# Moving the loads of three head pairs ahead of operand stores, and scaling keys last, in a fused retention and SwiGLU kernel

## The chip, the cores and the metric

The kernel runs on one core of one Trainium2 chip. The metric is the time of one execution on the device, in microseconds (us); lower is better. A core has a matrix engine (TensorE, PE in the profile, with its weight loads as PEld), VectorE (DVE), ScalarE (ACT), GpSimd (POOL) and SyncE (SP), each with its own queue of instructions that is worked off in order. In this kernel DMA transfers of the stage in question are issued from the queues of SP and of ACT.

## The reference

Two blocks, one after the other, all in float32. The first is retention: causal attention without softmax, with a decay per head.

```python
batch, n_heads, seq, head_dim = (8, 8, 576, 64)
scores = (1 / sqrt(64)) * q @ k.T                     # per batch and head
gamma = 1.0 - 2.0 ** (-5.0 - arange(8))               # one decay per head
D[i, j] = gamma ** (i - j) if i >= j else 0
attn = (scores * D) @ v
x = attn.transpose(0, 2, 1, 3).reshape(4608, 512)     # tokens x (heads, dims)
# SwiGLU feed-forward, d_model 512, d_ff 1536
g = x @ w_gate
out = (g * sigmoid(g) * (x @ w_val)) @ w_out          # 4608 x 512
```

## The kernel before

**Retention by pairs.** Two heads of one batch entry make a pair; there are 32 pairs, numbered `i`, four to a batch entry. A pair's sequence is handled in chunks of 64 positions. The work of a pair is spread over three calls of `tick(t)` (L595): at tick t, pair t is transposed and its keys are scaled (`transposes`, L428), pair t-1 gets its scores and states (`scores`, `new_states`, `masked`), and pair t-2 gets its outputs (`own_values`, `earlier_values`, `to_x`). The order of a tick's TensorE work is: `own_values(t-2)`, `new_states(t-1)`, `earlier_values(t-2)`, `scores(t-1)`. `new_states` needs the scaled keys `kn` of its pair, `scores` needs its `qT` and `kT`.

The vector work of a tick is put on a list, `pieces`, and taken off it a few at a time by `go_on(n)`, in this order: copies of the even states together with `keys` (the scaling of the pair's keys), then the outputs, then the mask of the scores, then the states, then the two transposes of `qT` and `kT`. `vector(i)` (L424) is true for pairs 0 and 10 to 12: their keys are scaled on VectorE. For pairs 4 to 9 ScalarE does it.

**Loads.** `load(i)` (L258) issues 13 transfers for a pair from 4 on: four for q and four for k in the layout that the transposes want (`qk`), two for k (`kn`), two for v, one for the last piece of v. They go out on SP's queue, except those of pair 11, which go out on ACT's queue (L267). The buffers rotate: `qk` has two places (`ld`, bufs=2), `kn` three, `v` four, so a load that is emitted waits until an earlier pair has left its place.

**The feed-forward.** Tokens 0 to 511 are computed in the plain way (`up0`, `down0`, `out0`). The other 4096 tokens are four tiles of 1024, and each of their products is done by a fast-matrix-multiplication scheme: three tables (UP, DOWN, OUT_SUMS) list sums and differences of blocks of the operands, 26 block products each, and how the products are added up. The 26 combinations of the weights `w_out` are the same for all tiles, so they are made once and written to DRAM (`dn_ops`, three column groups `qd` 0 to 2 of 26 blocks), and later fetched. This is `out_sums(qd)` (L707): for qd 0 and 1 the sums run on GpSimd and their stores go out on SP's queue; for qd 2 the sums run on VectorE and the stores go out on ACT's queue. A sum is kept in a place out of a short list (six places for GpSimd, six more from f=11 on), and a place is free again when the store of it has landed. `out_sums` returns nine groups of about three stores each.

**The order around the change.** It is written out by hand. A plan runs `up0(f)` for f = 2 to 11, with ticks 4 to 9 after f = 2, 3, 5, 7, 10, 11 (`tick_at`, L978). `next_load(t)` emits `load(t + 2)`. Of the groups of sums for qd 0 and 1, three each follow f = 7, 8, 10 and 11 (L989). Then a loop over twelve `down0` steps, numbered m (L999), runs ticks 10 to 13 after m = 1, 3, 6 and 8, `go_on(4)` in each step, the six groups that are left for qd 1, and the nine groups of qd 2, one for each m from 0 to 8. After m = 8 the sums of the x operands for the first tile of 1024 tokens begin on VectorE (`x_sums`); they need the outputs of pair 11, which come out of tick 13. The tile itself starts with `up_step` (L866) after `out0`.

On SP's queue the order around the change is therefore: load of pair 8, nine stores, load of pair 9, nine stores, load of pair 10, 34 stores. On ACT's queue: the last rounding of weights, the SiLU of `up0(11)`, the copies and keys of tick 9, the load of pair 11, 26 stores for qd 2.

A transfer also waits on one of eight completion counters that the transfers share in the order in which the program was laid out, so that a transfer is issued only when the one eight before it has landed, whichever queue that was on. In the profile such a wait is seen as a store that waits for the landing of a transfer to which it has no other relation.

Of the kernel before, what the change touches and what calls it, by code (L numbers as in the profile page):

```python
# [12 lines left out]
F32 = mybir.dt.float32  # L13
# [3 lines left out]
AF = mybir.ActivationFunctionType  # L17
ALU = mybir.AluOpType
# [136 lines left out]
def kernel(  # L155
# [32 lines left out]
    nc = tc.nc  # L188

    B, H, S, D = q.shape  # L190
    NT, DM = out.shape
    DF = moe_w_gate.shape[1]
    P = 128
    HP = H // 2
# [4 lines left out]
    SQ = 32  # L199
# [3 lines left out]
    NF = DF // P  # L203
# [6 lines left out]
    scale = 1.0 / math.sqrt(D)  # L210
# [4 lines left out]
    ld = ctx.enter_context(tc.tile_pool(name="ld", bufs=2))  # L215
# [26 lines left out]
    rest = const.tile([P, 17920], F32, name="rest")  # L242
# [15 lines left out]
    def load(i):  # L258

        b, p = divmod(i, HP)
        t = kp.tile([P, NFULL, 2, D], F32, tag="v", name="v", bufs=4)
        last = kp.tile([P, D], F32, tag="vl", name="vl", bufs=4)

        queues = (nc.sync, nc.scalar if i < 2 else nc.gpsimd if i < HP else nc.sync)
        if i >= HP and i == needed(1) - 3:  # L267

            queues = (nc.scalar, nc.scalar)

        def chunks(dst, src, hl):
            queues[hl].dma_start(out=dst[:, :, hl, :], in_=src[b, 2 * p + hl, 0:CW, :].rearrange("(c p) d -> p c d", p=P))

        if i < HP:

            late = [rest[:, dn_at + 1280 * (i - 2) + 640 * n :][:, 0:640] for n in range(2)] if i > 1 else None
            flat = late[0] if late else ld.tile([P, 2, S // SQ, SQ], F32, tag="qk", name="qk").rearrange("p n j d -> p (n j d)")
            qk = (flat[:, 0:CW].rearrange("p (c h d) -> p c h d", h=2, d=D),
                  flat[:, CW : CW + P].rearrange("p (h d) -> p h d", h=2))
            kn = (late[1][:, 0:CW].rearrange("p (c h d) -> p c h d", h=2, d=D) if late  # L280
                  else kp.tile([P, NFULL, 2, D], F32, tag="kn", name="kn"))
            for hl in range(2):
                chunks(qk[0], q, hl)
            for n, src in enumerate((q, k)):
                queues[n].dma_start(out=qk[1][half[n]], in_=src[b, 2 * p : 2 * p + 2, CW:S, :].rearrange("h p d -> p h d"))
        else:
            qk = ld.tile([P, 2, S // SQ, SQ], F32, tag="qk", name="qk")
            kn = kp.tile([P, NFULL, 2, D], F32, tag="kn", name="kn")
            for n, src in enumerate((q, k)):
                for a in range(P // SQ):  # L290
                    queues[0].dma_start(
                        out=qk[a * SQ : (a + 1) * SQ, n],
                        in_=src[b, 2 * p + a // 2, :, (a % 2) * SQ : (a % 2 + 1) * SQ].rearrange("(j t) d -> t j d", t=SQ))
        for dst, src in ((kn, k), (t, v)):
            for hl in range(2):
                chunks(dst, src, hl)
        if i < HP:
            for hl in range(2):
                queues[hl].dma_start(out=last[half[hl]], in_=v[b, 2 * p + hl, CW:S, :])
        else:  # L300
            queues[0].dma_start(out=last, in_=v[b, 2 * p : 2 * p + 2, CW:S, :])
        loaded[i] = (qk, kn, t, last)
# [13 lines left out]
    inv, key = tab[:, 0:H], tab[:, H : 2 * H]  # L316
# [103 lines left out]
    def light(i):  # L420

        return needed(1) - 2 <= i < needed(2) - 2

    def vector(i):  # L424

        return i == 0 or 10 <= i <= needed(1) - 2

    def transposes(i):  # L428
        p = i % HP
        qk, kn, vt, last = loaded.pop(i)  # L430
        qT = qp.tile([P, S], F32, tag="qT", name="qT")
        st[i] = dict(qT=qT, kn=kn, v=vt, last=last)
        pieces = []

        copy = nc.scalar.copy if i else nc.vector.tensor_copy
        if i < HP:

            for t, src, bank in ((qT, qk[0], bankA), (kT, kn, bankB)):
                for c in range(NFULL):
                    nc.tensor.transpose(bank[:, ts(c, P)], src[:, c].rearrange("p h d -> p (h d)"), ident)  # L440
                copy(t[:, 0:CW], bank)
            nc.tensor.transpose(bankC[:, 0:P], qk[1].rearrange("p h d -> p (h d)"), ident)
            for n, t in enumerate((qT, kT)):
                copy(t[:, CW:S], bankC[:, n * L : (n + 1) * L])
        else:
            if light(i):
                def scale_q():

                    src = qk[:, 0].rearrange("p (j r) d -> p r j d", r=2)
                    for r in range(2):  # L450
                        nc.scalar.activation(out=src[:, r], in_=src[:, r], func=AF.Copy, scale=piece[:, 2 * p + r : 2 * p + r + 1])
                pieces.append(scale_q)
            for n, t in enumerate((qT, kT)):
                pieces.append(lambda n=n, t=t: nc.vector.transpose(out=t, in_=qk[:, n].rearrange("p j d -> p (j d)")))

        def keys():
            for hl in range(2):
                if vector(i) or 1 < i < HP:
                    (nc.vector if vector(i) else nc.gpsimd).tensor_scalar(out=kn[:, :, hl, :], in0=kn[:, :, hl, :],
                                            scalar1=key[:, 2 * p + hl : 2 * p + hl + 1], scalar2=None, op0=ALU.mult)  # L460
                else:
                    nc.scalar.activation(out=kn[:, :, hl, :], in_=kn[:, :, hl, :], func=AF.Copy,
                                         scale=key[:, 2 * p + hl : 2 * p + hl + 1])

        if light(i):
            return [lambda: (keys(), pieces[0]())] + pieces[1:]
        return [keys] + pieces
# [125 lines left out]
    pieces = []  # L593
# [42 lines left out]
    def go_on(n):  # L636
        for _ in range(min(n, len(pieces))):
            pieces.pop(0)()

    def needed(n):  # L640

        last = (min(starts[n] + TW, NT) - 1) // S
        return last * HP + HP - 1 + 3
# [4 lines left out]
    def up0(f, chunks):  # L648

        pair = banks[2 * (f % 2) : 2 * (f % 2) + 2]  # L650
        for gv, bank in enumerate(pair):
            for c in chunks:
                nc.tensor.matmul(bank, w_up[:, f // 4, gv, f % 4, c // 2, (c % 2) * P : (c % 2 + 1) * P], xs[0][:, c, :],  # L653
                                 start=(c == 0), stop=(c == HP - 1))
        if HP - 1 in chunks:
            s = io[:, (f % 2) * T0 : (f % 2 + 1) * T0]
            nc.scalar.activation(out=s, in_=pair[0], func=AF.Silu)
            nc.vector.tensor_tensor(out=hid0[f], in0=pair[1], in1=s, op=ALU.mult)
# [43 lines left out]
    for line in OUT_SUMS:  # L702
        i, s = line.split("|")
# [259 lines left out]
    def next_load(t):  # L963
        if t + AHEAD < NP:
            load(t + AHEAD)
# [4 lines left out]
    plan = []  # L970

    def round_until(i):
        while todo and order.index(i) >= todo[0]:
            m = todo.pop(0)
            plan.extend(lambda j=j: rounding(j) for j in (2 * m, 2 * m + 1))

    round_until(3)
    tick_at = {2: 4, 3: 5, 5: 6, 7: 7, 10: 8, 11: 9}  # L978
    for f in range(2, NF):
        round_until({4: 12, 6: 13, 8: 14, 9: 15, 10: 16, 11: 17}.get(f, f + 2))  # L980
        plan.append(lambda f=f: up0(f, range(HP)))
        if f - 1 in tick_at and f < NF - 1:
            plan.append(lambda t=tick_at[f - 1]: next_load(t))
        if f in tick_at:
            plan.append(lambda t=tick_at[f]: tick(t, HP, FIRST))
        if f >= NF - 2:

            plan.append(lambda t=tick_at[f]: next_load(t))
        for _ in range(0 if f == 9 else 3):  # L989
            if f >= (7, 10, NF)[groups[0][0]]:  # L990
                if f + 1 == NF and more_places:
                    plan.append(lambda places=more_places[:6]: pool_places.extend(places))
                    more_places.clear()
                plan.append(lambda group=groups.pop(0)[1]: group())
# [3 lines left out]
    tick_at = {1: 10, 3: 11, 6: 12, 8: 13}  # L998
    for m, f in enumerate(down_order):  # L999
        down0(f)  # L1000
        go_on(4)
        if m in tick_at:
            tick(tick_at[m], HP, FIRST, tick_at[m] + 1 < needed(1))
            go_on(1)
        if m == 8:
            first_sums(0, 0, 4)
        if m > 8:
            x_sums(1, 3 * (m - 9), min(3 * (m - 8), X_FIRST), True)
        if groups:
            groups.pop(0)[1]()  # L1010
        if last_groups:
            last_groups.pop(0)()
# [58 lines left out]
```

## Time and profile before

| | |
|---|---|
| time, median of 3 runs | 1072.69 us (1072.22 to 1075.32) |
| span of the profiled execution | 1071.5 us |
| PE busy | 1040.9 us, 97% |
| DVE busy | 662.0 us, 62% |
| POOL busy | 394.4 us, 37% |
| ACT busy | 272.1 us, 25% |
| DMA packets under 512 B | 215352 of 300700 |

A share of busy time is over the whole span. PE is busy almost always, so the few places where it is not are what can be gained. The profile gives for each engine a timeline in which equal instructions are merged (start, duration, engine, line, what it writes and reads, count, and in brackets the idle time before it with what ended it), and the chain of work that ended last. A name such as `SPq L740` is a DMA issue from SP's queue; `DMA dn<-rest` is the transfer itself, here a store of a sum. `L689` is the line of the adds in the helper `add`, and is shared by all sums; what it writes tells which they are: `rest<-rest 128x256` are sums for w_out.

### The profile page before, as it was taken

What the parts mean: (1) busy time and instruction counts of PE and PEld (TensorE: products, weight loads), DVE (VectorE), ACT (ScalarE), POOL (GpSimd) and SP (SyncE); (2) the same over time, 40 slices, a digit from 0 to 9 for tenths busy, and PEclk for the clock granted to TensorE, in tenths of its full rate; (3) what the DMA queues carried; (4) which work ended last, traced back from release to release, by engine and by line L of the source; (5) the groups of instructions that cost most, each with busy time, mean ns of one, the idle gap of its engine ahead of it and who ended that gap; (6) DMA issues with size and microseconds to landing.
All of it is one profiled execution on the core that took longest, in us unless ns stands there. A gap on an engine that the chain in (4) does not pass through costs nothing.

```text
span 1071.5 us, 21458 instructions
## 1 busy us (share of the span) xinstructions
PE 1040.9 (97%) x8420; PEld 853.9 (80%) x8420; DVE 662.0 (62%) x1093; ACT 272.1 (25%) x578; POOL 394.4 (37%) x345
## 2 busy tenths in 40 slices
PE   6999989999999999999999999999999999999998
PEld 5454544788788788888888888888888888888887
DVE  4568777876968757562657868526276555244644
ACT  3555400224343220223222112132221022221110
POOL 5002454466464304731225026513150384123505
PEclk9999988999999999999999999999999999999999
DMA  9899797546676968756757777554564555555653
GB/s 255 235 264 247 199 234 201 171 148 200 162 205 179 255 173 223 213 180 182 192 133 225 186 223 206 154 153 134 155 176 150 158 180 154 150 155 155 189 157 99
DMA packets 300700, 198.58 MB, mean 185 GB/s; under 512 B 215352, under 2 KB 244056, under 8 KB 300600
## 3 DMA queue, kind: packets, MB, share of 16 engines
q1 hardware_dynamic: 264486, 155.75, 54.2%
q10 hardware_dynamic: 35698, 40.58, 11.4%
q8 instruction: 67, 1.10, 0.5%
q0 software_dynamic: 416, 0.89, 0.3%
q14 instruction: 33, 0.27, 0.1%
HBM read 157.04 MB, written 40.11 MB: 184 GB/s over the span
## 4 chain that ended last, share of the span: by engine, by line
PE 83%; DVE 5%; DMA 4%; POOL 3%; issue 1%; SPq 1%; ACT 0%; DVEq 0%; ACTq 0%; POOLq 0%
PE bankC L882 11%; PE bankE L882 11%; PE bankB L882 11%; PE bankA L882 11%; PE bankA L921 6%; PE bankE L921 6%; PE bankB L921 6%; PE bankC L921 6%; DVE rest L822 2%; PE bankA L653 2%; PE bankC L653 2%; PE bankB L653 2%; PE outer L504 2%; PE bankE L653 2%; POOL rest L689 1%; DMA dn<-rest 1%
## 5 line engine op out<-in xcount | busy, mean ns | idle before, releaser
L822 POOL TENSOR_TENSOR rest<-rest 128x512 f32<-128x512 f32 x56 | 79.1, 1419 | 299.5 <-DVE rest L822 278.4
L897 ACT ACTIVATE io<-rest 128x256 f32<-128x256 f32 x180 | 74.9, 416 | 340.9 <-DVE rest L822 294.8
L689 POOL TENSOR_TENSOR arena<-arena 128x512 f32<-128x512 f32 (+1 forms) x72 | 115.2, 1613 | 45.2 <-DMA up<-arena 24.4
L882 PE MATMUL bankC<-rest,arena 128*128 128x256 f32 x544 | 129.2, 381 | 0.5 <-DVE rest L822 0.5
L882 PE MATMUL bankA<-rest,arena 128*128 128x256 f32 x544 | 128.9, 380 | 0.4 <-DVE rest L822 0.4
L882 PE MATMUL bankE<-rest,arena 128*128 128x256 f32 x512 | 121.5, 380 | 0.6 <-DVE rest L822 0.6
L882 PE MATMUL bankB<-rest,arena 128*128 128x256 f32 x512 | 121.4, 380 | 0.4 <-DVE rest L822 0.4
L882 PEld LDWEIGHTS bankA<-rest,arena 128*128 128x128 f32 x544 | 103.3, 190 | 15.3 <-DVE rest L822 0.8
L882 PEld LDWEIGHTS bankC<-rest,arena 128*128 128x128 f32 x544 | 103.0, 190 | 15.3 <-issue 1.2
L904 POOL TENSOR_TENSOR arena<-rest,io 128x256 f32<-128x256 f32 x72 | 51.8, 726 | 167.0 <-ACT io L897 167.0
L882 PEld LDWEIGHTS bankB<-rest,arena 128*128 128x128 f32 x512 | 97.2, 190 | 14.1 <-DVE rest L822 0.8
L882 PEld LDWEIGHTS bankE<-rest,arena 128*128 128x128 f32 x512 | 97.1, 190 | 14.2 <-issue 1.0
L689 POOL TENSOR_TENSOR rest<-rest 128x256 f32<-128x256 f32 (+1 forms) x66 | 65.5, 1013 | 100.3 <-issue 59.3
L822 DVE TENSOR_TENSOR rest<-bankC,rest 128x512 f32<-128x512 f32 x72 | 48.9, 687 | 65.9 <-PE bankC L882 46.0
L822 DVE TENSOR_TENSOR rest<-bankB,rest 128x512 f32<-128x512 f32 x72 | 48.9, 687 | 64.6 <-PE bankB L882 46.5
L822 DVE TENSOR_TENSOR rest<-bankE,rest 128x512 f32<-128x512 f32 x72 | 48.8, 686 | 64.1 <-PE bankE L882 45.9
L822 DVE TENSOR_TENSOR rest<-bankA,rest 128x512 f32<-128x512 f32 x72 | 48.8, 686 | 61.2 <-PE bankA L882 43.9
L900 DVE SCALAR_TENSOR_TENSOR arena<-rest,io 128x256 f32<-128x256 f32 x84 | 57.1, 684 | 11.7 <-ACT io L897 11.2
L921 PE MATMUL bankA<-arena 128*128 128x256 f32 x252 | 58.0, 380 | 1.3 <-DVE arena L689 1.3
L921 PE MATMUL bankB<-arena 128*128 128x256 f32 x252 | 58.3, 382 | 0.0
L921 PE MATMUL bankC<-arena 128*128 128x256 f32 x252 | 58.1, 381 | 0.0
L921 PE MATMUL bankE<-arena 128*128 128x256 f32 x252 | 57.9, 380 | 0.0
(181 smaller groups left out, 1639.2 us busy)
## 6 DMA issues: line engine op xcount, KB each, us to landing
arena<-up SPq DMA_DIRECT2D x234, 256.0 KB
arena<-dn SPq DMA_DIRECT2D x104, 384.0 KB
up<-arena ACTq DMA_DIRECT2D x78, 256.0 KB
out_dram<-rest SPq DMA_DIRECT2D x32, 256.0 KB
qk<-in_q_dram SPq DMA_DIRECT2D x108, 72.0 KB
qk<-in_k_dram SPq DMA_DIRECT2D x108, 72.0 KB
v<-in_v_dram SPq DMA_DIRECT2D x58, 128.0 KB
kn<-in_k_dram SPq DMA_DIRECT2D x56, 128.0 KB
```

Source lines behind the costliest of these rows:

```text
L504: nc.tensor.matmul(xr[half[hl]] if c + 1 == NC else xo[half[hl ^ c % 2 * exchange(i)], c // 2, c % 2], state[half[hl], c, :], s["qT"][half ...
L653: nc.tensor.matmul(bank, w_up[:, f // 4, gv, f % 4, c // 2, (c % 2) * P : (c % 2 + 1) * P], xs[0][:, c, :], start=(c == 0), stop=(c == HP ...
L689: eng.tensor_tensor(out=dst, in0=srcs[0], in1=srcs[1], op=ALU.add if op[0] == "add" else ALU.subtract)
L822: eng.tensor_tensor(out=at(op[1]), in0=at(op[2]), in1=at(op[3]), op=ALU.add if op[0] == "add" else ALU.subtract)
L882: nc.tensor.matmul(b[:, gv * TB : (gv + 1) * TB], w[:, gv, ts(c, P)], rhs[:, c, :], start=(opens and gv == 0 and c == 0), stop=(c == 1), s ...
L897: nc.scalar.activation(out=s, in_=src[:, 0:TB], func=AF.Silu, scale=-1.0 if negative else 1.0)
L900: return lambda: nc.vector.scalar_tensor_tensor(out=dst, in0=src[:, TB : 2 * TB], scalar=-1.0, in1=s, op0=ALU.mult, op1=ALU.mult)
L904: nc.gpsimd.tensor_tensor(out=dst, in0=src[:, TB : 2 * TB], in1=s, op=ALU.mult)
L921: nc.tensor.matmul(b[:, m * TB : (m + 1) * TB], lhs[:, qd, ts(m, P)], w[:, qd], start=(opens and qd == 0 and m == 0), stop=(qd == NQ - 1), ...
```

## The change

Five edits that belong together:

1. `load(9)` is emitted right after tick 7 at f = 7, ahead of the first groups of sums, instead of at f = 8 behind them. `load(10)` stays after tick 8 at f = 10. `load(11)` is emitted before tick 9 at f = 11 instead of after it.
2. The groups of sums are spread as 3, 4, 5 over f = 7, 10, 11 instead of 3, 3, 3, 3 over f = 7, 8, 10, 11. There are still twelve.
3. The `qk` of pair 11 gets a place of its own in the arena `rest`, where a buffer of raw weights has been, so that its load does not wait for the transposes of pair 9.
4. For the pairs of `vector(i)` from 10 on, `keys` is taken out of the front of the pieces and put behind the transposes.
5. `go_on(5)` in place of `go_on(4)` in the loop over `down0`, since there is one piece more; so both transposes of a pair come before the sums of that step.

On SP's queue the order becomes: load of pair 8, load of pair 9, nine stores, load of pair 10, 43 stores. On ACT's queue: the SiLU of `up0(11)`, the load of pair 11, the copies and keys of tick 9, 26 stores.

It is meant to bring the data of pairs 9 to 11 early enough for their ticks, so that VectorE does not stand in front of keys that have not landed and the transposes do not stand behind sums.

```diff
@@ load @@
-            qk = ld.tile([P, 2, S // SQ, SQ], F32, tag="qk", name="qk")
+            if i == needed(1) - 3:
+                qk = rest[:, 4096 : 4096 + 2 * S].rearrange("p (n j d) -> p n j d", n=2, d=SQ)
+            else:
+                qk = ld.tile([P, 2, S // SQ, SQ], F32, tag="qk", name="qk")
@@ transposes (keys is defined earlier, unchanged) @@
             for n, t in enumerate((qT, kT)):
                 pieces.append(lambda n=n, t=t: nc.vector.transpose(out=t, in_=qk[:, n].rearrange("p j d -> p (j d)")))
+            if vector(i):
+                return [lambda: None] + pieces + [keys]
@@ the plan @@
-        if f - 1 in tick_at and f < NF - 1:
+        if f - 1 in tick_at and f < 7:
             plan.append(lambda t=tick_at[f - 1]: next_load(t))
+        if f == NF - 1:
+            plan.append(lambda t=tick_at[f]: next_load(t))
         if f in tick_at:
             plan.append(lambda t=tick_at[f]: tick(t, HP, FIRST))
-        if f >= NF - 2:
-
+        if f in (7, 10):
             plan.append(lambda t=tick_at[f]: next_load(t))
-        for _ in range(0 if f == 9 else 3):
+        for _ in range({7: 3, 10: 4, 11: 5}.get(f, 0)):
@@ the loop over down0 @@
         down0(f)
-        go_on(4)
+        go_on(5)
```

More of the change, by code (lines that the diff above doesn't have):

```diff
@@ L433, in transposes, with keys @@
         pieces = []
+        def keys():
+            for hl in range(2):
+                if vector(i) or 1 < i < HP:
+                    (nc.vector if vector(i) else nc.gpsimd).tensor_scalar(out=kn[:, :, hl, :], in0=kn[:, :, hl, :],
+                                            scalar1=key[:, 2 * p + hl : 2 * p + hl + 1], scalar2=None, op0=ALU.mult)
+                else:
+                    nc.scalar.activation(out=kn[:, :, hl, :], in_=kn[:, :, hl, :], func=AF.Copy,
+                                         scale=key[:, 2 * p + hl : 2 * p + hl + 1])
         copy = nc.scalar.copy if i else nc.vector.tensor_copy
@@ L454, in transposes @@
                 pieces.append(lambda n=n, t=t: nc.vector.transpose(out=t, in_=qk[:, n].rearrange("p j d -> p (j d)")))
[L456 to L463, printed above, removed]
+            if vector(i):
+                return [lambda: None] + pieces + [keys]
         if light(i):
```

## The prediction

> **What bounds the kernel now.** I read the page first, then TensorE's timeline for idle time, then the chain of waits around what I found, then the timelines of SP, GpSimd and VectorE there.
>
> ```profile
> PE 1040.9 (97%) x8420; PEld 853.9 (80%) x8420; DVE 662.0 (62%) x1093; ACT 272.1 (25%) x578; POOL 394.4 (37%) x345
> ```
>
> TensorE is the bound: 30.6 us of the span are idle. Outside the first 30 us the largest gaps are in the `down0` loop, at ticks 11 and 13 (TensorE's timeline):
>
> ```profile
> 146.16 0.70 PE L481 MATMUL outer<-ret,v 64*64 64x64 f32 x32 [0.57 <-DVE ret_last L532]
> 147.91 1.15 PE L504 MATMUL outer<-qT,state 64*64 64x64 f32 x32 [0.47 <-DVE state L539]
> 152.37 0.37 PE L511 MATMUL outer<-qT,kT 64*64 64x64 f32 x2 [3.32 <-DVE kT L454]
> 153.63 2.08 PE L665 MATMUL bankA<-rest,arena 128*128 128x512 f32 x2
> 178.39 0.70 PE L481 MATMUL outer<-ret,v 64*64 64x64 f32 x32 [1.99 <-DVE ret_last L532]
> ```
>
> Read the brackets: 0.57 + 0.47 + 3.32 = 4.36 us at tick 11, 1.99 (and 0.18 + 0.39 behind it) = 2.56 at tick 13. A pair of `down0` matmuls then takes 2.08 instead of 1.02 us: TensorE runs at half clock. The second gap is followed by the same (2.07 at 182.04). The table by windows gives the two stages together:
>
> ```profile
> 128.00:146.00 18.00, 17.59 (x210) 9.18 (x205) 11.20 (x29) 1.18 (x3) 7.29 (x9) 1.00 0.93 202
> 146.00:185.00 39.00, 32.50 (x384) 18.41 (x385) 29.48 (x63) 1.15 (x2) 23.03 (x29) 0.84 0.74 221
> ```
>
> The granted clock of 0.84 over 39.0 us is 0.16 x 39 = 6.2 us of lost full-clock time. With 6.9 us idle, 13.1 us is all that this region can give.
>
> VectorE says why tick 11 was late: keys of pair 10 that had not landed, and four sums between the two transposes.
>
> ```profile
> 142.32 0.35 DVE L459 TENSOR_SCALAR kn<-kn,tab 128x256 f32<-128x256 f32 x1 [3.31 <-DMA kn<-in_k_dram]
> 143.22 0.35 DVE L459 TENSOR_SCALAR kn<-kn,tab 128x256 f32<-128x256 f32 x1 [0.55 <-DMA kn<-in_k_dram]
> 148.46 3.16 DVE L689 TENSOR_TENSOR rest<-rest 128x256 f32<-128x256 f32 x4
> 151.55 0.76 DVE L454 STREAM_TRANSPOSE kT<-qk 128x576 f32<-128x576 f32 x1
> ```
>
> But the chain of waits does not go through tick 11. Through this time it runs over the stores and GpSimd's sums, and ends in tick 13:
>
> ```profile
> 144.13 4.10 DMA dn<-rest
> ...
> 153.28 3.75 POOL rest L689 x5
> ...
> 169.77 0.32 SPq L740
> 170.09 0.05 issue
> 170.14 2.18 DMA dn<-rest
> 172.32 0.02 issue
> 172.34 0.02 ACTq L740
> 172.36 0.04 issue
> 172.40 3.77 DMA dn<-rest
> ```
>
> After the last GpSimd sum a store of SP lands, lets a store of ACT go (shared counters), and that one frees a place for the VectorE sum at 176.26, which stands ahead of the mask that tick 13 needs. So what a faster tick 11 brings is given back at tick 13, unless GpSimd's sums end earlier. GpSimd itself stood still three times for a store's landing: 21.40 us before 114.18, 6.99 before 129.21, 11.63 before 148.37:
>
> ```profile
> 148.37 1.59 POOL L689 TENSOR_TENSOR rest<-rest 128x256 f32<-128x256 f32 x2 [11.63 <-DMA dn<-rest]
> ```
>
> **What the Trainium skill says.** "DMA: Bandwidth & Descriptors", Anatomy of one DMA: any wait for a semaphore happens on the issuing sequencer, before the transfer is handed over. The trace agrees: ACT is silent from 133.3 to 144.2 while it issues the 13 transfers of pair 11. The same page, Issuing engines are not separate DMA queues: transfers of all issuers share 16 DMA engines, and a second issuer saves only issue time. The trace has loads 10 and 11 side by side, at 10 us for the first against 7.6 us for load 9 alone. "TensorE: Matmul & The Clock Gate", What's actually happening: the clock is halved by an activity window of about 3.4 us. The trace's two half-clock stretches are 6.8 us each, after idle stretches of 3.32 and 1.99 us with small gaps beside them.
>
> **The change part by part.**
>
> *Loads 9 and 10 against stores (SP).* Nothing is removed from SP's queue; nine stores pass from before load 9 to behind it. SP is free of load 8 at 109.5 in both. Load 9's `qk` place is free after the transposes of pair 7 at 99.8, so it starts at 109.6. It took 7.6 us (118.2 to 125.8); I add the 2.4 us that SP stood at 111.0 for a weight transfer to land: 119 to 119.6. Nine stores took 8.5 us (109.62 to 118.1): to 127.6 or so. Load 10 (place free after the transposes of pair 8, 124.0) takes 7.6 to 9.5: 135 to 137. The next store feeds GpSimd 3.3 to 5.1 us later (125.89 to 129.21; 143.26 to 148.37): GpSimd resumes at 138.5 to 142.
>
> GpSimd's work: its four stretches are 5.97, 7.86, 7.32 and 21.92 us, of which 1.3 is a sum for another stage; 41.8 us. By the resumption the first two are done (three groups and six places ahead, as at 122.2 before). 28 us remain, against 20.6 at 148.4 before. End: 166.5 to 170, against 169.7; I take 167.7, 2.0 us earlier. The gain is small because the queue has the same content: the stall before load 10 is shorter, but the first stall is longer, since load 9 now stands in it.
>
> *From there to tick 13.* 169.7 to 178.39 is 8.7 us of store, store, sum, mask. With the same 8.7 tick 13 starts at 176.4. If ACT's stores come to stand before more of SP's last stores in the shared order (GpSimd has more left in this region), the coupling shortens by about two stores of 0.8 us each. I take 175.3, gain 3.1.
>
> *Load 11 ahead of tick 9 (ACT), with a place of its own.* It starts after the SiLU at 123.2 in place of 133.3. Queued behind it: the copies of pair 8 (128.84 before) and keys of pair 9. 13 issues at 0.55 us are 7.2 us; at the 10.9 us it took before it ends at 134.1. The vector work behind the copies needs 0.4 + 1.9 (states) + 1.45 (transposes) = 3.7 us, and `scores(9)` is at 137.8: copies may come as late as 134.1. So 0 to 1 us of wait at tick 10; I take 0.
>
> *Keys last, transposes ahead of sums.* From 138.6 to 152.3 VectorE took 13.7 us for tick 10, 3.9 of it the wait for keys. 9.8 remain: all done at 148.4, with keys last instead of `kT`. TensorE comes to `new_states(10)` at 146.1 and waits 2.3 us for them, in place of 4.36. Load 10 ends seven us earlier, so no landing is waited for. The same edit at tick 12 leaves about 1 us of wait for keys 11, since 12 us of vector work stand against 12.9 us of TensorE's. TensorE so reaches tick 13 at 172 (full clock after tick 11) or 174 (half clock).
>
> *Clock.* Of 6.2 us, one stretch of 3.0 may go: if the clock is halved at tick 11, tick 13 has only 1 us to wait and keeps it; if not, it waits 3 us and is halved there. Of the second gap's 3.6 us (3.0 clock, 0.6 small gaps) I count 1.1.
>
> *The rest* (respread groups, `go_on(5)`, pair 12's keys on VectorE two steps later) moves no work; slack of several steps hides it. Later tiles shift with TensorE.
>
> Sum: 3.1 + 1.1 = 4.2; 1072.7 - 4.2 = 1068.5.
>
> **The rivals.** *TensorE stays fed:* the coupling of stores loosens so far that tick 13 does not wait. For it: VectorE's own group of sums there is done by about 166. Gain 7 to 13 us: 1060 to 1066. Against it: stores of ACT waited for SP's last ones at 172.3. *Nothing moves:* the new issue of load 11 sits among stores in the shared order; stores wait until ACT gets to it, GpSimd ends at 169.7 again, a clock drop remains: 1071 to 1073. *Slower:* the same, worse: nine stores held from 121 to 127 by load 11, load 10 later, GpSimd at 173 or later, or ACT's copies past 134 so that ticks 10 and 11 both stand: +3 to +6 us, 1076 to 1079. For it: GpSimd has 28 us left when load 10 ends, and 21.40 us of idle time become about 30. Against it: SP's 13 issues are the same.
>
> **How the numbers follow.** Forecast 0.42 (1066.5 to 1069.5), fed 0.16, nothing 0.18, slower 0.24. Bounds: 1062 cuts off the far half of the fed case, 1077 about half of the slower one. Faster by over 0.3% (under 1069.5), forecast and fed: 0.58; within 0.3%: 0.18; slower 0.24.
>
> **What would show it.** SP: load 9 directly behind load 8, from 109.6; then nine stores and load 10 ending near 136. GpSimd: one long stall to about 123, one near 131 to 140, end at 166 to 170. ACT: load 11 from 123.2. VectorE: no idle time before the keys of pair 10. TensorE: a wait of 2 to 3 us in tick 11 for keys, ended by L459, and a tick 13 at 174 to 177. Wrong if tick 13 comes at its own time without a wait, or if GpSimd ends after 170.

## The result and the profile after

The changed kernel takes 1083.39 us (median of 4 runs, 1081.23 to 1084.02), the kernel before 1073.82 us (4 runs, 1072.22 to 1075.32). The ratio is 1.0086, with a 95% interval of 1.0062 to 1.0109: slower by 0.9%, about 9 us, where 4 us of gain were predicted.

The first line is the page's busy time by engine after the change; it hardly differs from before. What differs is where the idle time lies.

```profile
PE 1041.4 (96%) x8420; PEld 854.2 (79%) x8420; DVE 666.2 (62%) x1093; ACT 271.9 (25%) x578; POOL 394.7 (37%) x345
```

To find it, cut the span at two events that both kernels have: the first TensorE instruction of tick 7 and the first product of tile 1 (`up_step`). The table by windows (columns: window, its length, busy time of PE, PEld, DVE, ACT, POOL with counts, granted TensorE clock, DMA share, GB/s) of the kernel before, cut there:

```profile
92.70:194.40 101.70, 94.78 (x1045) 51.02 (x1046) 73.01 (x151) 21.09 (x39) 40.44 (x51) 0.93 0.78 208
194.40:1071.50 877.10, 865.32 (x6465) 757.18 (x6463) 533.07 (x818) 204.37 (x453) 333.67 (x262) 1.00 0.62 176
```

and of the changed kernel:

```profile
94.50:203.10 108.60, 94.55 (x1045) 52.77 (x1045) 70.75 (x151) 21.05 (x39) 40.71 (x51) 0.92 0.74 198
203.10:1081.00 877.90, 865.78 (x6465) 755.57 (x6463) 539.25 (x819) 204.50 (x453) 333.57 (x262) 1.00 0.61 175
```

The stage grew by 6.9 us. TensorE is busy in it for as long as before (94.55 against 94.78 us) with the clock at 0.92 against 0.93, so the 6.9 us are idle time: 14.05 against 6.92 us. After the stage there is 0.8 us of difference. Another 1.8 us lie ahead of tick 7 (94.5 against 92.7), where the order is the same in both; in ten kernels that share it tick 7 comes anywhere from 92.5 to 95.3 us, so no cause is sought for that.

The idle time is seen in TensorE's timeline of the changed kernel (start, length, line, operands, count; in brackets the idle time before it and what ended it), at ticks 10, 11 and 13:

```profile
146.42 1.13 PE L486 MATMUL outer<-ret,v 64*64 64x64 f32 x32 [8.74 <-DVE ret_last L537]
151.32 1.65 PE L670 MATMUL bankA<-rest,arena 128*128 128x512 f32 x2
...
162.69 0.47 PE L495 MATMUL inner<-v,kn 64*64 64x64 f32 x2 [3.09 <-DVE kn L441]
...
188.44 0.69 PE L486 MATMUL outer<-ret,v 64*64 64x64 f32 x32 [1.24 <-DVE ret_last L537]
```

Tick 10, which did not wait before, now waits 8.74 us for the mask that VectorE makes. The pair of `down0` matmuls behind it took 1.65 us where 1.02 is the usual length: the granted clock was halved until 152.4. One step back, VectorE's timeline says what the mask waited for:

```profile
145.54 0.69 DVE L529 TENSOR_TENSOR ret<-inner,near 128x512 f32<-128x512 f32 x1 [14.47 <-ACT even L533]
```

VectorE stood 14.47 us for the copies of pair 8, which are ACT's. ACT's timeline gives the cause:

```profile
124.56 1.99 ACTq L294 DMA_DIRECT2D rest<-in_q_dram  x4
126.64 7.35 ACTq L294 DMA_DIRECT2D rest<-in_k_dram  x4
138.82 1.55 ACTq L272 DMA_DIRECT2D kn<-in_k_dram  x2
141.44 2.06 ACTq L272 DMA_DIRECT2D v<-in_v_dram  x2
143.62 1.42 ACTq L304 DMA_DIRECT2D vl<-in_v_dram  x1
145.14 0.37 ACT L533 COPY even<-inner 128x256 f32<-128x256 f32 x1 [20.05 <-DMA vl<-in_v_dram]
```

`ACTq` lines are issues of transfers. Load 11 begins right behind the SiLU, at 124.56, as it was meant to. Its 13 issues then take until 145.04: 20.5 us, most of it standing. The copies came at 145.14, against 128.84 before. SP's timeline around them shows the other end:

```profile
117.83 0.98 SPq L272 DMA_DIRECT2D kn<-in_k_dram  x2
118.86 8.05 SPq L272 DMA_DIRECT2D v<-in_v_dram  x2
127.01 0.54 SPq L304 DMA_DIRECT2D vl<-in_v_dram  x1
127.65 8.26 SPq L745 DMA_DIRECT2D dn<-rest  x9
135.99 2.08 SPq L294 DMA_DIRECT2D qk<-in_q_dram  x4
138.12 2.12 SPq L294 DMA_DIRECT2D qk<-in_k_dram  x4
140.34 0.98 SPq L272 DMA_DIRECT2D kn<-in_k_dram  x2
```

The two queues are meshed through the completion counters. In the order in which the program was laid out, load 11's first q transfer stands eight places ahead of load 9's second v transfer. SP therefore stopped in the middle of load 9. The waits of SP's queue between 108 and 200 us (line, what it waited for, us in total, times, longest) name a transfer of ACT's:

```profile
SPq L272 <- DMA rest<-in_q_dram: 7.2, 1, 7.2
```

The meshing works the other way too. Load 11's later k transfers stand behind the end of load 9 and behind stores of SP; its kn, v and last piece stand between the transfers of load 10, which in time come after nine stores. So ACT could issue kn only at 138.82, when load 10's first transfers, issued from 135.99 on, were landing. It was issued 80 ns after the last update of its counter, the other late ones about 15 to 60 ns after theirs. The DMA engines were not full meanwhile: their busy share was 0.54 from 134.0 to 138.8, against 0.78 over the stage of the kernel before, so ACT did not stand for want of bandwidth.

The Trainium skill, "DMA: Bandwidth & Descriptors", Anatomy of one DMA, says that a wait for a semaphore is spent on the issuing sequencer, and this trace agrees. What it adds is the size of such waits on a queue that also computes: ACT ran no compute instruction for 20.05 us.

### The profile page after: what moved, and what is told of

It reads as the page before. It is cut to its first block, busy times and chain, and to the rows that moved or that the text cites. A ratio compares the mean times of both kernels' runs of the same rounds, so it can differ in the third digit from the quotient of the medians.

```text
span 1081.0 us, 21458 instructions
## 1 busy us (share of the span) xinstructions
PE 1041.4 (96%) x8420; PEld 854.2 (79%) x8420; DVE 666.2 (62%) x1093; ACT 271.9 (25%) x578; POOL 394.7 (37%) x345
## 4 chain that ended last, share of the span: by engine, by line
PE 80%; DVE 6%; DMA 4%; POOL 4%; issue 2%; SPq 1%; ACT 0%; ACTq 0%; DVEq 0%; POOLq 0%
PE bankC L887 11%; PE bankE L887 11%; PE bankB L887 10%; PE bankA L887 10%; PE bankA L926 6%; PE bankB L926 6%; PE bankE L926 6%; PE bankC L926 6%; DVE rest L827 3%; PE bankA L658 2%; POOL rest L694 2%; PE bankC L658 2%; PE bankB L658 2%; PE outer L509 2%; PE bankE L658 2%
```

## The experiments

Ratios are to the kernel before, measured on the same chip with each group of runs (medians 1074.6 and 1074.86 us); intervals are 95%. "Stage" is the window from tick 7 to tile 1 as above. The last two columns are times in the profiled execution, counted from the first TensorE instruction of tick 7: when tick 13 begins on TensorE, and when GpSimd's last sum for w_out ends.

| kernel | us | ratio | stage us | PE idle in it | tick 13 | GpSimd's end |
|---|---|---|---|---|---|---|
| before | 1073.82 | 1 | 101.7 | 6.92 | 85.8 | 77.1 |
| after (the change) | 1083.39 | 1.0086 (1.0062 to 1.0109) | 108.6 | 14.05 | 93.9 | 82.9 |
| e1: change, load 11 behind tick 9 | 1065.6 | 0.991 (0.9889 to 0.9932) | 92.6 | 3.10 | 79.9 | 79.6 |
| e2: load 11 early, alone | 1079.53 | 1.004 (1.0029 to 1.0052) | 106.7 | 14.73 | 94.2 | 78.8 |
| e3: loads 9 and 10 early, alone | 1069.39 | 0.9948 (0.9928 to 0.9968) | 97.8 | 5.68 | 80.4 | 81.4 |
| e4: keys last, alone | 1068.26 | 0.9933 (0.9912 to 0.9955) | 95.4 | 4.29 | 80.6 | 77.1 |
| e5: change, load 11 split | 1066.88 | 0.9923 (0.9898 to 0.9948) | 93.3 | 2.85 | 78.6 | 85.7 |
| e6: e1 without the own place | 1066.16 | 0.9916 (0.9894 to 0.9938) | 90.9 | 2.06 | 77.5 | 84.4 |
| e7: e1, keys before sums | 1065.75 | 0.9906 (0.9879 to 0.9932) | 89.2 | 0.85 | 75.9 | 82.7 |
| e8: before, more places | 1070.52 | 0.9953 (0.994 to 0.9967) | 97.1 | 4.92 | 84.6 | 78.3 |

Theory A: the early load 11 ties the two queues together; it is held on ACT, with the copies of pair 8 behind it, and it holds load 9 on SP. Theory B: the stores of SP that came behind loads 9 and 10 hold GpSimd, and GpSimd's end sets tick 13.

**e1: load 11 back behind tick 9.**

```diff
-        if f == NF - 1:
-            plan.append(lambda t=tick_at[f]: next_load(t))
         if f in tick_at:
             plan.append(lambda t=tick_at[f]: tick(t, HP, FIRST))
-        if f in (7, 10):
+        if f in (7, 10, 11):
             plan.append(lambda t=tick_at[f]: next_load(t))
```

> The changed kernel, with the load of pair 11 emitted behind tick 9 again; its own place, the loads of pairs 9 and 10 ahead of stores, and keys last stay. Theory A (the load of pair 11, put ahead of tick 9, ties the queues of SP and ACT together through the shared completion order: SP's load of pair 9 stood 7.2 us for it, and ACT's copies of tick 9 came 16 us late): no wait of 8.7 us at tick 10, the load of pair 9 runs through to about 120, GpSimd's sums end at 168 to 171, time 1068 to 1074 us. Rival B (putting loads ahead of stores on SP starves GpSimd, whatever ACT does): GpSimd still ends at 175 or later, time 1079 us or more.

17.8 us less than the changed kernel, and below the 1068 to 1074 expected. Load 9 runs through to 119.1, ticks 10 and 13 do not wait, tick 11 waits 1.71 and 0.47 us for keys, and the granted clock of the stage is 1.00 (the table by windows of e1, same columns as above):

```profile
93.00:185.60 92.60, 89.50 (x1045) 48.29 (x1045) 72.85 (x151) 21.03 (x39) 41.22 (x51) 1.00 0.81 221
```

Of the 9.1 us that its stage is shorter than before, 5.3 are PE busy time (89.50 against 94.78, at a granted clock of 1.00 against 0.93) and 3.8 idle time. GpSimd's end is 172.6, later than the 168 to 171 expected and, counted from tick 7, 2.4 us later than before, in a kernel that is 9 us faster. So an early load 11 is what cost the time; which of its two holds, SP's or ACT's, this run does not say.

**e2: load 11 early with its own place, in the kernel before, nothing else.**

```diff
             plan.append(lambda t=tick_at[f - 1]: next_load(t))
+        if f == NF - 1:
+            plan.append(lambda t=tick_at[f]: next_load(t))
         if f in tick_at:
...
-        if f >= NF - 2:
+        if f == NF - 2:
```

> The kernel before, with one part of the change: the load of pair 11 ahead of tick 9, with its own place. SP's order of loads and stores is that of before. Theory A: ACT begins the load at about 123 and is held by SP's load of pair 10, which is laid out between its transfers; the copies of tick 9 come at about 140 in place of 128.8, tick 10 waits 4 to 7 us, time 1076 to 1083 us. Rival B: SP's order is that of before, so 1071 to 1075 us.

Slower than before by 0.4%. ACT's timeline of e2, below it SP's, and TensorE's at tick 10:

```profile
126.09 2.66 ACTq L294 DMA_DIRECT2D rest<-in_k_dram  x4
140.13 1.38 ACTq L272 DMA_DIRECT2D kn<-in_k_dram  x2
...
146.44 0.37 ACT L531 COPY even<-inner 128x256 f32<-128x256 f32 x1 [22.15 <-DMA v<-in_v_dram]
```

```profile
137.27 2.08 SPq L294 DMA_DIRECT2D qk<-in_q_dram  x4
139.39 2.12 SPq L294 DMA_DIRECT2D qk<-in_k_dram  x4
```

```profile
147.72 1.13 PE L484 MATMUL outer<-ret,v 64*64 64x64 f32 x32 [10.85 <-DVE ret_last L535]
```

Load 11 is cut by a pause from 128.75 (126.09 + 2.66) to 140.13, between its k and kn transfers, although loads 9 and 10 and the stores stand on SP's queue in the order of before. It ends once load 10's transfers are under way on SP. The copies come at 146.44, not at about 140, and tick 10 waits 10.85 us, more than the 4 to 7 expected. So moving load 11 is enough to make the hold, and the new place of loads 9 and 10 is not needed for it.

**e3: loads 9 and 10 early and the groups respread, load 11 where it was.**

```diff
-        if f - 1 in tick_at and f < NF - 1:
+        if f - 1 in tick_at and f < 7:
...
-        if f >= NF - 2:
-
+        if f in (7, 10, 11):
             plan.append(lambda t=tick_at[f]: next_load(t))
-        for _ in range(0 if f == 9 else 3):
+        for _ in range({7: 3, 10: 4, 11: 5}.get(f, 0)):
```

> The kernel before, with the loads of pairs 9 and 10 ahead of stores and the groups of sums spread 3, 4, 5; the load of pair 11 as before, keys first. Theory A: GpSimd resumes at about 123 and 140 and ends at 167 to 171, time 1068 to 1074 us. Rival B: GpSimd ends at 175 or later, 1079 us or more.

Faster than before by 0.5%. The wait at tick 11 is gone (0.29 us), and tick 13 waits longer than before (TensorE's timeline of e3; 0.18 and 1.33 us follow):

```profile
175.69 1.13 PE L481 MATMUL outer<-ret,v 64*64 64x64 f32 x32 [3.89 <-DVE ret_last L532]
```

GpSimd ends at 176.7, later than the 167 to 171 expected and, counted from tick 7, 4.3 us later than before, and the kernel is still faster. Theory B falls with this: GpSimd does end late, but the time does not follow it.

**e4: keys last and `go_on(5)`, loads as before.**

```diff
+            if vector(i):
+                return [lambda: None] + pieces + [keys]
...
-        go_on(4)
+        go_on(5)
```

> The kernel before, with keys last in pairs 10 to 12 and five pieces a step, nothing else. Theory A: the wait at tick 11 falls from 4.4 us to about 2 to 3 us, ended by the keys; the end of GpSimd's sums and tick 13 do not move, time 1070 to 1074 us. Rival C (keys last is itself a loss, since new_states needs them earlier in a tick than scores needs the transposes): tick 11 waits longer than before, 1075 us or more.

Better than expected. Two lines of VectorE and one of TensorE, of e4, show why:

```profile
147.06 1.51 DVE L691 TENSOR_TENSOR rest<-rest 128x256 f32<-128x256 f32 x4
148.49 0.61 DVE L438 TENSOR_SCALAR kn<-kn,tab 128x256 f32<-128x256 f32 x2
```

```profile
148.89 0.89 PE L492 MATMUL inner<-v,kn 64*64 64x64 f32 x29 [0.17 <-DVE kn L438]
```

The four sums and the keys took 2.12 us here, since GpSimd stood still until 150.81. In e1, with GpSimd summing from 144.12, the same work takes longer (VectorE's timeline of e1):

```profile
144.96 2.58 DVE L694 TENSOR_TENSOR rest<-rest 128x256 f32<-128x256 f32 x4
147.47 1.61 DVE L441 TENSOR_SCALAR kn<-kn,tab 128x256 f32<-128x256 f32 x2
```

So tick 11 is met nearly in time in e4 (0.17 us of wait) and waited for in e1 (1.71 + 0.47 us): the 2.07 us by which sums and keys take longer are the 2.0 us by which it waits longer. Tick 13 waits 3.05 us in e4, with GpSimd done at 172.2; counted from tick 7 GpSimd ends when it did before, and tick 13 comes 5.2 us earlier.

**e5: the change, with load 11 split.** The eight q and k transfers stay ahead of tick 9; kn, v and the last piece (five transfers) go behind it.

```diff
-    def load(i):
+    def load(i, parts=(0, 1)):
...
-            plan.append(lambda t=tick_at[f]: next_load(t))
+            plan.append(lambda t=tick_at[f]: load(t + 2, (0,)))
...
+        if f == NF - 1:
+            plan.append(lambda t=tick_at[f]: load(t + 2, (1,)))
```

> The changed kernel, with only the eight q and k transfers of pair 11 that the transposes read (the ones that fill its own place) ahead of tick 9; its keys, values and last piece are emitted behind tick 9. ACT then has 8 transfers ahead of the copies of tick 9 in place of 13; the eight still stand in the shared order ahead of the end of SP's load of pair 9. If the loss is in the copies (ACT held): copies at 132 to 135, tick 10 waits under 1 us, time 1064 to 1070 us. If the loss is in SP's queue (load of pair 9 held 7 us, GpSimd late): GpSimd resumes at about 130 and ends at 176 to 178 as in the changed kernel, tick 13 waits for the sums, 1076 to 1083 us.

1066.88 us, close to e1. ACT's timeline of e5, TensorE's at tick 13, and the waits of its SP queue:

```profile
124.88 7.26 ACTq L296 DMA_DIRECT2D rest<-in_k_dram  x4
132.23 0.37 ACT L537 COPY even<-inner 128x256 f32<-128x256 f32 x1 [8.90 <-DMA dn<-rest]
```

```profile
171.33 0.69 PE L490 MATMUL outer<-ret,v 64*64 64x64 f32 x32 [1.32 <-DVE ret_last L541]
```

```profile
SPq L273 <- DMA rest<-in_q_dram: 7.2, 1, 7.2
```

SP's hold of 7.2 us is as long as in the changed kernel, and GpSimd's last of these sums ends at 178.4, later than the change's 177.4. But the copies come at 132.23, inside the 134.1 that the prediction allowed, and tick 10 does not wait. This separates the two holds. ACT's hold of the copies is worth the 16.5 us between e5 and the change, which both have the hold on SP. SP's hold may be worth 1 to 2 us: tick 13 waits 1.32, 0.18 and 0.55 us in e5 and only 0.18 in e1, and the two kernels' intervals overlap.

**e6: e1 without the own place** for the `qk` of pair 11 (it takes one of the two of `ld` again).

> The kernel of the load of pair 11 behind tick 9, without the place of its own for pair 11 (its load waits for the transposes of pair 9 again). If the place is worth nothing there: the same time within 0.3%, 1063 to 1068 us. If the early start of that load matters: 1069 us or more.

1066.16 against 1065.6 us, with intervals that nearly coincide. Behind tick 9 the place is worth nothing that these runs can tell.

**e7: e1 with `go_on(6)`**, so that the keys come before the sums of that step.

```diff
-        go_on(5)
+        go_on(6)
```

> The kernel of the load of pair 11 behind tick 9, with six pieces a step in place of five, so that the keys too come ahead of that step's sums on VectorE. The wait of 2.2 us for the keys at tick 11 and that of 0.5 us at tick 12 go: 1062 to 1065 us. If VectorE only passes the delay on to the sums and they hold tick 13 through their places: no change, 1065 to 1067 us.

In its trace the waits of ticks 11 to 13 are gone (0.85 us of idle time in the stage). The time is 1065.75 us, missing the expected 1062 to 1065 and not to be told from e1; it lies in the 1065 to 1067 of the second case, but not for the reason given there, since tick 13 does not wait. The stage is 3.4 us shorter than in e1, but 2.3 of it are given back after tile 1 has begun (879.0 us of span from there against 876.7), and the runs lie from 1060.9 to 1068.5. A late GpSimd is part of this: in e5, e6 and e7 its sums for w_out end only 6.5 to 7.7 us before tile 1 starts, and TensorE then waits 1.31, 0.87 and 1.12 us for GpSimd's next work; in e1, with 13.0 us between them, it does not.

**e8: the kernel before, with four more places for VectorE's sums.**

```diff
-    vector_places = x0_places + more_places[6:]
+    vector_places = x0_places + more_places[6:] + [rest[:, raw_at + 4096 + TB * i : raw_at + 4096 + TB * (i + 1)] for i in range(4)]
```

> The kernel before, with four more places for the sums that VectorE makes for qd 2 (18 in place of 14), nothing else. If tick 13 waits for places that ACT's stores free only after SP's last stores, as the chain of waits of before was read: no wait for stores on VectorE at 174 and 176, tick 13 comes at its own time or with under 1 us of wait, 1066 to 1070 us. If GpSimd's sums hold tick 13 in another way: 1072 to 1075 us.

TensorE's timeline of e8 at tick 13, and VectorE's sums ahead of it:

```profile
177.04 0.69 PE L481 MATMUL outer<-ret,v 64*64 64x64 f32 x32
```

```profile
170.46 2.82 DVE L689 TENSOR_TENSOR rest<-rest 128x256 f32<-128x256 f32 x4
```

No bracket on either: with places to spare the four sums run at once and tick 13 waits for nothing, although GpSimd ends at 170.8, 1.2 us later than before when counted from tick 7. The tie at tick 13 was the place of a VectorE sum that an ACT store had to free, and that store was laid out behind SP's last ones. GpSimd's end mattered only through this tie. The time, 1070.52 us, is just above the 1066 to 1070 expected: tick 11 still waits 1.83, 0.47 and 2.44 us.

## Why the prediction was wrong

**The step that failed** is "Load 11 ahead of tick 9": its sentence "13 issues at 0.55 us are 7.2 us; at the 10.9 us it took before it ends at 134.1" and the value taken from it, "I take 0". The 13 issues took 20.5 us, the copies came 11 us past the 134.1 allowed, and tick 10 waited 8.74 us. The duration was copied from a place in the order where ACT's issues ran side by side with those of load 10. Moved ahead, four of load 11's thirteen issues (kn and v) wait, through the shared counters, for transfers of load 10 that come behind nine stores on SP, and the last k waits for one of these stores. The wait was also ended at another point than the one that 134.1 was worked out from: not by `scores(9)`, but by the mask that `own_values(8)` needs, 1.28 us after the copies began. The prediction knew the coupling and used it for SP waiting on ACT (the second half of the rival "Slower": "nine stores held from 121 to 127 by load 11"; from 119.36 to 126.54 it was the second v transfer of load 9 that stood, with the nine stores behind it). It did not walk the same order from ACT's side, where the queue also carries the copies. What supports this reading is the trace, where the late issues follow their counters' updates within 80 ns, with e2 and e5. A kernel that changes the shared order alone and leaves both queues as they are was not tried.

**The rival "Slower"** had the mechanism in its last clause, ACT's copies past 134 so that ticks 10 and 11 both stand, at 1076 to 1079. The size was too small: copies at 145.14 gave 8.74 + 3.09 us at these ticks.

**A second wrong step: what a faster tick 11 brings "is given back at tick 13, unless GpSimd's sums end earlier".** The prediction took the chain of waits of the kernel before to hold in the changed order, with "the same 8.7" us from GpSimd's end to tick 13. Counted from tick 7, GpSimd ended at the same time as before in e4 and 2.4, 4.3 and 8.6 us later in e1, e3 and e5, yet tick 13 came 5.2 to 7.2 us earlier in all four. In e5 GpSimd ended 7 us after tick 13 had begun (171.33). e8 takes the wait at tick 13 away with GpSimd no earlier. The chain was read rightly for the kernel before, but three lines of it (store of SP, store of ACT, sum on VectorE) were a tie through a place, and could be cut without any gain on GpSimd. GpSimd's end itself was forecast too early. In e1, where SP is not held, load 10 takes 12.6 us (127.07 to 139.64) beside load 11 on ACT, where 7.6 to 9.5 were written, and GpSimd resumes at 144.12, not at 138.5 to 142. In the changed kernel it resumes at 148.28, with SP's hold of 7.2 us ahead of it, and ends at 177.4, outside "166.5 to 170".

**What was right.** Load 9 began behind load 8 (111.03) and had 11 of its 13 transfers out by 119.36, against 119 to 119.6 for the whole; nine stores took 8.26 us (8.5 predicted); load 10 took 8.2 us (7.6 to 9.5). The gain of the keys is real and larger than written: e4 alone gives 0.7%, e3 alone 0.5%. The parts of the change without the early load 11 are e1, 0.9% faster than before, which is the rival "TensorE stays fed" (1060 to 1066). The forecast's sum had discounted that gain by giving it back at tick 13.

**The clock.** Busy time tells that the change lost as much to the half clock as before (94.55 against 94.78 us), in three stretches of about 10.2, 3.4 and 3.4 us against two of 6.8: of the first, from 142.2 to 152.4, TensorE was idle until 146.42, and idle time loses no clock. The Trainium skill, "TensorE: Matmul & The Clock Gate", What's actually happening, gives a window of 3413 ns; the stretches are one, two and three of these to within 0.01 us. Idle stretches that are shorter than the window were enough here: 1.32, 0.18 and 0.55 us at tick 13 of e5 were followed by 3.4 us at half clock, while in e1 the gaps of 1.71 and 0.47 us at tick 11 cost no clock at all. What tells the two cases apart is not shown.

## What to carry to other kernels

Before moving a transfer forward on a queue that also computes, write down what each of its issues can wait for, including the transfer that its completion counter served before (here eight places earlier in the shared order, on whatever queue it is), and what stands behind it. In this kernel a load on ACT cost time when its pieces waited for SP's transfers and a copy that was due stood behind them. If only part of a load must be early, split it: e5 moved five of thirteen transfers back and regained 16.5 us. Test a chain of waits by cutting one tie of it (one more place, one store elsewhere) before working on the engine that it names.

## What the hardware showed

GpSimd slows VectorE while both sum. Four 128x256 sums of VectorE took 1.51 us with GpSimd standing still in e4, 2.58 us in e1 and 3.16 us in the kernel before with GpSimd at work; two scalings of keys took 0.61 us in e4 and 1.61 us in e1. Over the ten traces, from 90 to 190 us, a sum took 0.38 to 0.43 us with GpSimd idle (70 sums) and 0.83 us in the middle with GpSimd busy (108 sums), while a transpose of kT took 0.73 to 0.77 us in either case. The Trainium skill, "GPSIMD Engine Reference", Key points, says that GpSimd shares its SBUF interfaces with VectorE and contends with those of its instructions that run in a 2-port mode or have two SBUF inputs; the sums have two, and for four of them these runs put the factor at 1.7 to 2.1. A GpSimd that waits therefore has a use: it was one reason why e4, with loads as before, hardly waited at tick 11.

A transfer can wait for another queue's transfer whose data it has no use for: the 7.2 us of SP in the changed kernel, and the pause of 11.4 us in e2's load 11, were both such waits on a shared counter.
